# Moving two late x products and three y@w_ch products in a fused attention and spectral-mix kernel

## The chip, the cores and the metric

The kernel runs on one core of one Trainium2 chip. The time is the device time of one execution in microseconds (us). The profile's span is some 1.8 us shorter than the time of the same execution. All timed runs named here are of the same (fast) state, or single runs whose state isn't known; those are named.

The engines go by short names: PE multiplies matrices, DVE and ACT compute on and copy tiles (an *eviction* is a copy of a tile that PE wrote), POOL (GpSimd) issues the weight loads, SP the other DMAs. PE's granted clock is 1.00 or 0.50 in the records of these traces; 0.50 is called half clock. A load *lands* when its data are there.

## The reference, cut to what matters

```python
def reference(...):                      # q, k, v: (8, 8, 576, 64); w_r, w_i: (64, 512, 512); w_ch: (512, 512)
    x = attention(q, k, v, s)            # to (batch 8, sequence 576, 512)
    X = rfft(x, axis=1)[:, :64]          # 64 modes
    Y = X * (w_r + i w_i), mode by mode  # 64 products of (8, 512) by (512, 512), complex
    y = irfft(Y, n=576, axis=1)
    u = x + y
    return u + max(u @ w_ch, 0)
```

The product u @ w_ch is split: x @ w_ch and y @ w_ch. The second is cheap before the inverse transform, since Y has only 2 x 64 rows for each batch.

## The kernel before

The weights w_r and w_i (81.8 MB with q, k and v) are loaded on GpSimd's queue in 128 loads of 512 KB (as they land), and the last group of them is worked off in eight chunks of eight modes, four loads each. After each chunk its Y (`yb`, 128 rows: 16 of each of 8 batches) is transposed. Then there is a tail: for each pair of row tiles, the inverse transform of Y and of Y @ w_ch is added to x and to x @ w_ch. For that, both have to be laid out by batch in `yv`. That is done in two ways: by matmuls that pick one batch's columns out of the transposed Y (`gather`), or by a copy on SP (`spread`, 128 KB).

```python
    def spread(c, which, rows):
        nc.sync.dma_start(out=yv[16 * c : 16 * c + 16, :, which, :], in_=rows)
    # ... in modes(): for the last two chunks  spread(c, 0, yb)

    def y_times_wch(c, yt):
        # four matmuls 128x512 into v_ps, one DVE copy to v_sb
        spread(c, 1, vb)
        return vb

    def gather(c0, c1, turns, kinds):
        n = 2 * MC * (c1 - c0)               # 64 rows for four chunks, 32 for two
        ng = P // n                          # 2 or 4 batches share a PSUM tile
        for b0 in range(0, B, ng):
            for which in kinds:              # 1: @ w_ch, 0: as it is
                ps = auxpool.tile([P, DM], FP32, name="g_ps", tag="aux")      # two buffers
                # ... matmuls, ng column groups at once
                for g in range(ng):
                    # ... odd g on VectorE, even g on ScalarE, into yv
            if b0 // ng in turns:
                work()

    def work():                              # one late x product
        # transposes the next pair of x tiles; multiplies the pair before it by w_ch and keeps it

    TAKE = (3, 2, 2, 0, 1, 1)                # late products in chunks 0 to 5
    # ...
    for c in range(NCK - 2):                 # chunks 0 to 5
        yb = modes(NG - 1, c)
        for x in range(TAKE[c] - 1):
            work()
        # ...
        yt = y_transposed(yb, c)
        if TAKE[c]:
            work()
        if c >= NY:                          # chunks 4 and 5
            y_times_wch(c, yt)
            if c == NCK - 3:
                gather(NY, NCK - 2, (), (0,))
        elif c == NY - 1:                    # chunk 3
            gather(0, NY, (1, 3), (1, 0))
    # ... chunk 6: modes, transposes, vb6 = y_times_wch(6, yt)
    # ... chunk 7: modes, with the first pair's matmuls between its four loads
    # ... tail: 18 pairs; the third is the first to need all of yv
```

The softmax here doesn't subtract the row's maximum and nothing guards it: scores larger than these inputs give would overflow.

## Time and profile before

| | us |
|---|---|
| median of 3 runs | 456.54 (456.02 to 457.24) |
| span of the profiled execution | 453.8 |
| last weight load lands | 415.2 |
| chunk 7's last four mode products start | 415.30 |
| from there to the end | 38.5 |

The page names the engines' busy time, the chain that ended last, and the DMA queues. The prediction shows the lines on which its argument rests. Three lines of the page that it did not use are shown here, since they also belong here: the first, with the number of instructions, and two of the part on queues (packets, megabytes, share of the engines).

```profile
span 453.8 us, 10370 instructions
...
q8 instruction: 33, 0.54, 0.4%
q14 instruction: 14, 0.11, 0.1%
```

The program itself is read by DMA, in 33 packets of 16 KB on one queue and 14 of 8 KB on another. This is 0.5% of the engines' time and looks like nothing.

The next two lines are of the view of the tile `yv`, for the last copy of a v (chunk 7's): the issue (minimum, median and maximum in ns, then its time) and its time to landing.

```profile
L466 SPq DMA_DIRECT2D yv<-v_sb x1: 547/547/547, 418.7 to 418.7; - x1
...
DMA to landing us min/median/max: 2.9/2.9/2.9
```

### The profile page before, as it was taken

The page shows a single profiled execution, that of the slowest core. Times are in us where ns is not written, and L with a number is a line of the kernel's source. Part 1 is how long each engine was busy: PE and PEld are TensorE (multiplying, and loading weights), DVE is VectorE, ACT ScalarE, POOL GpSimd, SP SyncE. Part 2 cuts the span into 40 slices and gives each one's busy share as a digit, 9 for nine tenths or more (in the row PEclk, how much of TensorE's full clock was granted, in tenths as well). Part 3 has the DMA queues.
Part 4 walks back from the last instruction along what each step waited for, and adds up shares of the span by engine and source line. Part 5 has one row for each costly group of instructions (what it writes and reads, how often), then busy time and mean ns, then how long its engine had stood idle before and what let it go on. Part 6 is the DMA issues. An engine that isn't in the chain of part 4 may idle for free.

```text
span 453.8 us, 10370 instructions
## 1 busy us (share of the span) xinstructions
PE 340.4 (75%) x4233; PEld 218.6 (48%) x4265; DVE 241.0 (53%) x535; ACT 221.9 (49%) x390; POOL 183.0 (40%) x269
## 2 busy tenths in 40 slices
PE   1779887976563979836677857688889678879995
PEld 1456665654342656624445535456554335534332
DVE  7775665753242656723436434446655443562796
ACT  1585877464242656724435444455551323431774
POOL 6655554554344565434364444444433231200000
PEclk9996999998576889968878899889996986999999
DMA  9999999999999999999999999999999999995688
GB/s 176 200 203 203 202 201 204 202 204 204 205 204 202 201 203 202 205 205 204 202 196 203 204 204 203 204 203 202 206 207 208 207 206 206 207 214 109 232 298 317
DMA packets 108511, 93.75 MB, mean 207 GB/s; under 512 B 28384, under 2 KB 103648, under 8 KB 108464
## 3 DMA queue, kind: packets, MB, share of 16 engines
q0 software_dynamic: 98960, 81.81, 113.8%
q1 hardware_dynamic: 9504, 11.29, 7.8%
q8 instruction: 33, 0.54, 0.4%
q14 instruction: 14, 0.11, 0.1%
HBM read 164.56 MB, written 9.44 MB: 383 GB/s over the span
## 4 chain that ended last, share of the span: by engine, by line
DMA 51%; PE 31%; DVE 8%; issue 4%; POOL 2%; ACT 2%; SPq 0%; DVEq 0%; POOLq 0%; ACTq 0%
DMA w_sb<-in_moe_w_i_dram 21%; DMA q<-in_q_dram 15%; DMA w_sb<-in_moe_w_r_dram 11%; PE sc_ps L365 4%; PE av_ps L394 4%; PE z_ps L602 3%; PE yp L441 3%; PE sc_ps L359 3%; PE tr_ps L324 3%; DMA k<-in_k_dram 2%; PE z_ps L693 2%; PE g_ps L652 2%; PE ft_ps L418 2%; PE u_ps L712 2%; PE u_ps L693 1%
## 5 line engine op out<-in xcount | busy, mean ns | idle before, releaser
L373 ACT ACTIVATE p_sb<-sc_ps,cumt_sb 128x576 f16<-128x576 f32 (+1 forms) x256 | 141.7, 635 | 45.6 <-PE sc_ps L365 45.0
L217 POOL DMA_DIRECT2D w_sb<-in_moe_w_i_dram x60 | 45.1, 751 | 85.0 <-PE yp L441 37.6
L217 POOL DMA_DIRECT2D w_sb<-in_moe_w_r_dram x60 | 45.3, 757 | 63.5 <-DMA w_sb<-in_moe_w_r_dram 28.2
L217 POOL DMA_DIRECT2D v<-in_v_dram x72 | 50.8, 708 | 32.0 <-DMA w_sb<-in_moe_w_r_dram 7.4
L324 PE MATMUL tr_ps<-ident,q 64*64 64x64 bf16 x576 | 17.5, 210 | 54.3 <-DMA q<-in_q_dram 54.3
L359 PE MATMUL sc_ps<-negm,ident 128*128 128x256 bf16 x256 | 55.5, 303 | 0.2
L327 DVE COPY qtA<-tr_ps 64x576 bf16<-64x576 bf16 x32 | 23.8, 743 | 49.6 <-PE tr_ps L324 49.5
L441 PE MATMUL yp<-w_sb,xs 128*32 128x512 bf16 x480 | 36.5, 406 | 14.1 <-DMA w_sb<-in_moe_w_i_dram 11.1
L344 ACT ACTIVATE p<-sc_ps,cumt 128x64 f16<-128x64 f32 x32 | 10.0, 313 | 74.3 <-PE sc_ps L340 74.3
L394 PE MATMUL av_ps<-v,p_sb 128*128 128x65 f16 x1024 | 44.5, 198 | 0.0
L394 PEld LDWEIGHTS <-p_sb 128*128 128x128 f16 x1024 | 39.5, 100 | 4.9 <-issue 0.8
L327 DVE COPY ktA<-tr_ps 64x576 bf16<-64x576 bf16 x32 | 24.0, 749 | 33.6 <-PE tr_ps L324 33.6
L324 PEld LDWEIGHTS <-q 64*64 64x64 bf16 x576 | 13.7, 123 | 57.0 <-DMA q<-in_q_dram 56.3
L365 PE MATMUL sc_ps<-qtB,ktB 128*128 128x64 bf16 (+2 forms) x160 | 34.9, 324 | 3.5 <-issue 2.4
L365 PE MATMUL sc_ps<-qtA,ktA 65*128 65x512 bf16 (+2 forms) x192 | 36.5, 299 | 0.7 <-DMA qtA<-ncum_sb 0.7
L399 DVE TENSOR_REDUCE den<-av_ps 128x5 f32<-128x10 f32 x64 | 10.8, 169 | 49.1 <-PE av_ps L394 48.9
L441 PEld LDWEIGHTS <-xs 128*32 128x32 bf16 x512 | 22.6, 170 | 23.8 <-issue 19.8
L404 DVE TENSOR_TENSOR x_all<-av_ps,rcp 128x320 f16<-128x320 f32 x64 | 31.5, 491 | 2.2
L327 ACT COPY ktB<-tr_ps 64x576 bf16<-64x576 bf16 x32 | 20.3, 634 | 20.3 <-DVE ktA L327 19.4
L365 PEld LDWEIGHTS <-ktB 128*128 128x128 bf16 x192 | 22.4, 117 | 14.8 <-issue 6.3
L324 PE MATMUL tr_ps<-ident,k 64*64 64x64 bf16 x576 | 17.3, 209 | 15.3 <-DVE qtB L327 10.7
L602 PE MATMUL z_ps<-wch_sb,xs 128*128 128x512 f16 x96 | 26.1, 421 | 0.2 <-DVE xs L596 0.2
(117 smaller groups left out, 534.8 us busy)
## 6 DMA issues: line engine op xcount, KB each, us to landing
w_sb<-in_moe_w_r_dram POOLq DMA_DIRECT2D x60, 512.0 KB, 11.9
w_sb<-in_moe_w_i_dram POOLq DMA_DIRECT2D x60, 512.0 KB, 11.9
q<-in_q_dram POOLq DMA_DIRECT2D x32, 144.0 KB, 9.9
k<-in_k_dram POOLq DMA_DIRECT2D x32, 144.0 KB, 10.0
v<-in_v_dram POOLq DMA_DIRECT2D x72, 64.0 KB, 9.7
out_dram<-r_sb SPq DMA_DIRECT2D x16, 256.0 KB, 2.2
out_dram<-r_w SPq DMA_DIRECT2D x16, 256.0 KB, 2.6
x_all<-in_moe_w_i_dram POOLq DMA_DIRECT2D x3, 512.0 KB, 9.9
```

The costliest lines, as they stand in the source:

```text
L217: nc.gpsimd.dma_start(out=dst, in_=src)
L324: nc.tensor.transpose(ps[rows, r, :], src[rows, r, :], ident16[rows, rows])
L327: copy(out=dst[n % NQ][rows, :].rearrange("d (p r) -> d p r", r=R), in_=ps[rows].rearrange("d r p -> d p r"),)
L359: nc.tensor.matmul(ps[:, bass.ds(w * S, W)], ident16, negm[:, bass.ts(r, W)], start=True, stop=False, skip_group_check=True,)
L365: nc.tensor.matmul(ps[:, c0 : c0 + i1 - i0], keys[:, w, r, :], qt[:, i0:i1], start=False, stop=True, skip_group_check=True,)
L373: nc.scalar.activation(out=pt[:, poff[x] : poff[x] + S - w * W], in_=ps[:, w * S : (w + 1) * S - w * W], func=ACTF.Exp, bias=cumt_sb[:, x, ...
L394: nc.tensor.matmul(ps[:, I, r : r + NCH], lhsT, rhs, start=(i == 0), stop=(i == len(todo) - 1), skip_group_check=True,)
L399: nc.vector.tensor_reduce(out=den, in_=ps[:, :, 0 : VW : NCH], axis=mybir.AxisListType.X, op=ALU.add)
L404: nc.vector.tensor_tensor(out=x_all[:, g, b, :, D * h : D * h + D], in0=ps[:, :, 1 : NCH], in1=rcp.unsqueeze(2).to_broadcast([P, NT, D]), ...
L441: nc.tensor.matmul(ps[32 * cg : 32 * cg + 32, :], cols[:, c0 : c0 + 32, c * MC + 2 * cg + par], wt[(g, c, ri, par)][:, cg, :], start=(x == ...
L602: nc.tensor.matmul(z[:, x, :], xts[i][:, x, dt, :], wch_sb[:, dt, :], start=(dt == 0), stop=(last and dt == DT - 1), skip_group_check=True,)
L693: nc.tensor.matmul(dst[x][r, :], G_sb[rows, bass.ds(T * P, r.stop - r.start)], yv[rows, bb, which, :], start=start, stop=True, skip_group_ ...
```

## The change

It takes PE work off the stretch after the last chunks' loads, and copies off the stream of loads. (The change's title counts chunks from one; this text, like the code, from zero.) Two late x products move to chunks 0 and 1. The v of chunks 4 and 5 are gathered, like their y, in four column groups, with the rounds spread over the code. Chunk 6's v copy is issued behind chunk 7's y. In a gather, the last piece of a tile goes to DVE and all others to ACT.

```diff
@@ y_times_wch
-        spread(c, 1, vb)
         return vb
@@ gather(c0, c1, r, which): now one tile of one round
+        for g in range(ng):
+            dst, src = yv[rows, r * ng + g, which, :], ps[n * g : n * g + n, :]
+            if g == ng - 1:
+                nc.vector.tensor_copy(out=dst, in_=src)
+            else:
+                nc.scalar.copy(out=dst, in_=src)
@@
-    TAKE = (3, 2, 2, 0, 1, 1)
+    TAKE = (4, 3, 2, 0, 0, 1)
@@ for c in range(NCK - 2)
-        if c >= NY:
-            y_times_wch(c, yt)
-            if c == NCK - 3:
-                gather(NY, NCK - 2, (), (0,))
-        elif c == NY - 1:
-            gather(0, NY, (1, 3), (1, 0))
+        if c == NY - 1:
+            for r in range(4):
+                gather(0, NY, r, 1)
+                gather(0, NY, r, 0)
+                if r == 3:
+                    work()
+        elif c == NCK - 3:
+            gather(NY, NCK - 2, 0, 1)
+            gather(NY, NCK - 2, 0, 0)
     c = NCK - 2
     x_times_wch(0, False)
+    gather(NY, NCK - 2, 1, 1)
     yb6 = modes(NG - 1, c)
     x_transposed(1)
+    gather(NY, NCK - 2, 1, 0)
     # ...
     yb = modes(NG - 1, NCK - 1, {2: first_u, 3: first_z})
+    spread(NCK - 2, 1, vb6)
```

More of the change, by code (lines that the diff above doesn't have):

```diff
@@ L637, in y_times_wch, with gather @@
         nc.vector.tensor_copy(out=vb, in_=vp)
-        spread(c, 1, vb)
         return vb
-    def gather(c0, c1, turns, kinds):
+    def gather(c0, c1, r, which):
         n = 2 * MC * (c1 - c0)
@@ L645, in gather @@
         ng = P // n
-        for b0 in range(0, B, ng):
-            for which in kinds:
-                ps = auxpool.tile([P, DM], FP32, name="g_ps", tag="aux")
-                for dt in range(DT):
-                    for g in range(ng):
-                        op = yt_first[:, dt, : c1 - c0].rearrange("p c (x b) -> p (c x) b", b=B)
-                        nc.tensor.matmul(
-                            ps[n * g : n * g + n, :] if which else ps[n * g : n * g + n, bass.ts(dt, P)],
-                            op[:, :, b0 + g],
-                            wch_sb[:, dt, :] if which else ident16h,
-                            start=(dt == 0 or not which), stop=(dt == DT - 1 or not which),
-                            tile_position=(0, n * g), skip_group_check=True,
-                        )
-                for g in range(ng):
-                    dst, src = yv[rows, b0 + g, which, :], ps[n * g : n * g + n, :]
-                    if g % 2:
-                        nc.vector.tensor_copy(out=dst, in_=src)
-                    else:
-                        nc.scalar.copy(out=dst, in_=src)
-            if b0 // ng in turns:
-                work()
+        ps = auxpool.tile([P, DM], FP32, name="g_ps", tag="aux")
+        op = yt_first[:, :, : c1 - c0].rearrange("p d c (x b) -> p d (c x) b", b=B)
+        for dt in range(DT):
+            for g in range(ng):
+                nc.tensor.matmul(
+                    ps[n * g : n * g + n, :] if which else ps[n * g : n * g + n, bass.ts(dt, P)],
+                    op[:, dt, :, r * ng + g],
+                    wch_sb[:, dt, :] if which else ident16h,
+                    start=(dt == 0 or not which), stop=(dt == DT - 1 or not which),
+                    tile_position=(0, n * g), skip_group_check=True,
+                )
+        for g in range(ng):
+            dst, src = yv[rows, r * ng + g, which, :], ps[n * g : n * g + n, :]
[3 more added lines that the diff above has]
+                nc.scalar.copy(out=dst, in_=src)
     ahead = []
```

## The prediction

> **What bounds the kernel now.** I read the page's slices first, then the chain that ended last in order of time, then the issues of the weight loads with their time to landing, then the busy table in short windows.
>
> From the page, 40 slices of 11.3 us each:
>
> ```profile
> PE   1779887976563979836677857688889678879995
> PEclk9996999998576889968878899889996986999999
> GB/s 176 200 203 203 202 201 204 202 204 204 205 204 202 201 203 202 205 205 204 202 196 203 204 204 203 204 203 202 206 207 208 207 206 206 207 214 109 232 298 317
> ```
>
> The transfers run at a flat 200 to 208 GB/s for 36 slices while PE is never full. Only the last four slices (from 408 us) look different. So up to about 410 us the kernel is a stream of loads, then comes a tail without loads. The chain in order of time (start, length, what) gives another impression:
>
> ```profile
> 353.00 19.81 DMA w_sb<-in_moe_w_i_dram
> 372.80 0.04 issue
> 372.85 0.59 PE yp L441 x4
> ...
> 377.51 0.59 ACT yv L664
> 378.10 0.02 issue
> 378.12 0.70 DVE yv L662
> 378.83 0.04 issue
> 378.87 2.42 PE g_ps L652 x15
> ...
> 414.94 0.43 PE z_ps L702 x2
> 415.38 0.43 PE yp L441 x4
> ```
>
> After the load that landed at 372.8 the chain names no transfer any more: from there to the last chunk's last four matmuls (415.38) it is PE with ACT and DVE copies. Read alone, this says that all PE work after 372.8 us is on the path, and moving work ahead of it should pay in full. I do not believe that, because of the last loads. Issues on POOL, with start, length and idle time before:
>
> ```profile
> 391.58 0.74 POOL L217 DMA_DIRECT2D w_sb<-in_moe_w_i_dram  x1 [9.86 <-PE yp L441]
> 392.31 0.75 POOL L217 DMA_DIRECT2D w_sb<-in_moe_w_r_dram  x1
> 393.23 0.74 POOL L217 DMA_DIRECT2D w_sb<-in_moe_w_r_dram  x1 [0.17 <-PE yt_ps L625]
> 393.96 0.76 POOL L217 DMA_DIRECT2D w_sb<-in_moe_w_i_dram  x1
> 396.87 0.74 POOL L217 DMA_DIRECT2D w_sb<-in_moe_w_i_dram  x1 [2.15 <-PE yp L441]
> ```
>
> For the last one the tile view gives
>
> ```profile
> DMA to landing us min/median/max: 18.3/18.3/18.3
> ```
>
> so it lands at 396.87 + 18.3 = 415.17 us, and the first matmul that needs it starts at 415.30. Asked one by one, the last landings are 400.8 (issued 380.98 + 19.8), 404.3, 406.2, 409.3, 412.0 and 415.2. **Two paths meet at 415.2**: PE's own work, and the stream of loads. Taking work from PE alone gains almost nothing; the stream must shorten too.
>
> The POOL gap of 9.86 us looks alarming but starved nothing: four loads were still to land, and the windows table keeps its DMA share of 1.24 and 203 to 210 GB/s throughout the gap.
>
> **What the Trainium skill says.** "DMA: Bandwidth & Descriptors", section "Issuing engines are not separate DMA queues": transfers started from sync or gpsimd run on the same 16 DMA engines and interleave. So a copy of v into yv (128 KB, issued on SP) takes time from the weight stream. The trace agrees: undisturbed loads land 2.5 us apart (19.8 us latency, issues 2.53 us apart), but the last five took 415.2 - 400.8 = 14.4 us, not 5 x 2.53 = 12.65. In that time four such copies were in flight (issued 398.2, 402.6, 407.7, 411.9). That is 1.75 us for four, **0.44 us each**.
>
> "TensorE: Matmul & The Clock Gate", section "What's actually happening": PE runs at half clock after an idle activity window of about 3.4 us and at full clock after a busy one; the windows are free-running. The trace agrees. In windows of 1 us the granted clock is 0.50 from 342.3 to 349.1, 362.9 to 366.2 and 373.05 to 383.3; the edges all fit a period of 3.41 us. From 373 to 380 PE was some 59 and 71% busy (2.0 and 2.4 us of each window) and stayed slow; 379.9 to 383.3 was full (the late product at 381.3 filled it) and freed it.
>
> "PSUM — Partial Sum Buffer", section "PSUM bank collisions raise a hardware error": two engines must not touch the same bank and quadrant together; different quadrants may. The pieces of a gather are in different quadrants, but this kernel's DVE copies still follow the ACT ones (378.10, then 378.12), as the chain shows; I expect that order to stay.
>
> **The change part by part.** The instruction order before and after shows the same 247 GpSimd rows in the same order, so the loads themselves are unchanged; PE has 48 more (32 products and 32 weight loads added, 8 and 8 removed), SP two copies fewer.
>
> *Two late x products.* They go from the first gather (after r=1) and from chunk 4 to chunks 0 and 1. Each is 8 transposing matmuls (0.62 us) and 8 of 128x512 (1.73 us): 2.35 us at full clock. Before, PE sat idle around 359 to 363 and 371 to 373 us waiting for loads, so they fit there: chunk 1 ends at 357.9 + 4.7 = 362.6, and chunk 2's last load lands at 362.5. This may even spare the half clock at 362.9. Chunk 3 still ends with the load of 372.8. Off PE's path after 372.8: 4.7 us.
>
> *y@w_ch of chunks 4 and 5.* Removed: 2 x 4 matmuls (0.86 us each, 1.7 in all), two DVE copies of 0.69 and two SP copies. Added: two gathers of 16 matmuls of 128x32 weights, four column groups at once. The same form in the mode products costs 1.1 us for 16 (the timeline at 390.79: 1.12), so 2.2 us. Evictions: the gather of these chunks had two tiles with four pieces each, half on ACT and half on DVE; now it has four tiles, with three pieces of each on ACT and one on DVE: 3 x 0.58 + 0.70 = 2.4 us per tile, with two tiles in rotation. The four tiles cost about 9.7 us of copying between 398 and 409 us, mostly beside x products and waits. PE: +0.5 us. **Stream: two copies fewer.**
>
> *Chunk 6's v copy* (called chunk seven in the title, counting from one) now is issued behind y7's, after the last load. **One copy fewer ahead of the last landing.** Its consumer is the third pair's z at 421.99. The v7 copy, issued at 418.72, needs 2.9 us: 421.6. So there is only 0.35 us of slack, and an extra copy in flight could eat 0 to 0.3 us.
>
> *The stream's sum*: 3 x 0.44 = **1.3 us**. Last landing 415.2 - 1.3 = 413.9.
>
> *PE's sum*: 4.7 - 0.5 = 4.2 us less work, but not all is gained. With no product between its rounds the first gather waits for its copies. One round at full clock is 1.13 (PE) + 0.59 + 0.70 + 0.1 = 2.5 us; at half clock, as here from 373 us, about 3.4. Four rounds from 375.5: the last starts near 385.6 and its PE work ends at 388. In the windows 376.5 to 386.7 PE is then about 73% busy, as in the one that did not free the clock, so I expect half clock until about 390.1. Then the single product to 391.3, chunk 4 to 393.2, chunk 5 modes to 394.7 (before: 397.2), and carrying the rest on at full clock, with 2.4 us of eviction between gathers, PE is ready for the last four matmuls at about 413.5 (before: 415.3). So PE is ready about when the load lands, with little to spare.
>
> Sum: the end comes **1.3 us earlier, less 0.1** for the v copies: 456.54 - 1.2 = 455.3.
>
> **The rivals.**
>
> A: *PE is the bound, as the chain says.* Then 4.2 us less gives 452.3. For it: no transfer in the chain after 372.8. Against: the landing at 415.17 allows at most the shortening of the stream. I give it little.
>
> B: *A new PE delay.* The half clock holds longer (another 3.4 us window costs some 1.7 us), or ACT's twelve small evictions hold back the copy of chunk 6's transpose and so v6 and the first z. For it: my schedule has about 0.4 us of spare, and the windows' phase differs from run to run. It would make 455.5 to 457.5.
>
> C: *The copies were hidden.* The GB/s rose to 227 and 228 in the windows 402 to 404 and 406 to 408 us, so part of a copy is additional. Then the landing moves by only 0.5 us: 456.
>
> D: *Too much slack.* If PE idles over 2 us before the last load, the tail starts at half clock, +1.7 us. At 413.5 against 413.9 I don't expect it.
>
> **Range and chances.** The middle is 455.4, a little above the sum because B and C both push up. The copy's price alone (0.2 to 0.6 each) gives 454.7 to 456; B adds up to 2 us; the runs before spread by 1.2 us. Range 454.2 to 456.9. 2% is 9.1 us: faster would need more than all PE work moved, slower would need five extra half-clock windows.
>
> **What would show it.** Last weight landing at 413.5 to 414.3, and the last five landings 12.7 to 13.3 us apart in all. Chunk 4's mode products at 390 to 392 us with clock 0.5 up to about 390. PE waiting under 1 us for the last load, or the chain naming that load between 400 and 414. The stretch from the last mode matmul to the end unchanged at 38.0 us (415.81 to 453.8). The prediction is wrong if the last landing stays at 415 (C), if PE starts the last four over 0.5 us after their landing (B), or if the tail is longer than 38.4 us (the v copies).

## The result

The changed kernel took 457.26 us (median of 6 runs, 456.36 to 457.7), the kernel before 456.21 us on the same chip (6 runs, 455.56 to 457.24). The ratio is 1.0019, with a 95% interval of 1.0004 to 1.0035. A ratio is the mean time of one kernel's fast runs over that of the other's of the same rounds, so it is not quite the ratio of the medians. The change is within 2%, but it costs time, and the time lies above the range that was given.

The page after, its first line and three lines of its slices:

```profile
span 455.3 us, 10449 instructions
...
PE   1779997976553979836678788789888966889994
...
PEclk9995999997777799967769768799995995799999
...
GB/s 170 199 202 203 202 201 203 203 204 204 205 204 202 199 200 203 205 205 204 202 193 203 204 204 204 204 204 202 207 206 208 208 205 206 206 207 93 231 304 296
```

The page counts 79 instructions more; 32 of these are matmul records that are missing before (4233 matmuls against 4265 weight loads), and PE really has 48 more. The stream is as flat as before up to the 37th slice, in which it ends. The chain that ended last, in order of time:

```profile
386.63 2.42 PE g_ps L649 x14
389.06 0.97 PE xt_ps L592 x8
390.02 2.97 PE z_ps L602 x8
...
404.34 0.58 ACT yv L661
404.92 0.02 issue
404.94 0.71 DVE yv L659
405.65 0.04 issue
405.69 1.15 PE yp L441 x16
...
415.94 0.43 PE yp L441 x4
...
419.29 3.49 DMA yv<-v_sb
422.78 0.05 issue
422.83 0.60 PE z_ps L688 x2
```

Three things are new. The gather's last round starts at 386.6 and the product after it runs mostly at half clock (eight matmuls in 2.97 us; at full clock 1.73). Before chunk 6's mode products at 405.69 stand a row of ACT copies and a DVE copy, not a load. And after the last chunk the chain goes through the copy of v7, 3.49 us, where before it went through matmuls. The view of `yv` agrees; it gave 2.9 before:

```profile
DMA to landing us min/median/max: 3.5/3.5/3.5
```

The last load, from the issues on POOL and the view of its tile:

```profile
397.06 0.74 POOL L217 DMA_DIRECT2D w_sb<-in_moe_w_i_dram  x1 [0.22 <-issue]
...
DMA to landing us min/median/max: 18.0/18.0/18.0
```

It landed at 415.0 us, and the four matmuls that need it started at 415.87, where before the two were 0.1 us apart.

**Where the time went.** The landing records of the trace let the span be cut into five terms that don't depend on one another: until chunk 0's last load has landed (before any changed instruction), from there to the sixth landing from the end, the last five landings, the gap until the last four mode products start, and the rest.

| term, us | before | changed | difference |
|---|---|---|---|
| until chunk 0's last load | 342.16 | 343.30 | +1.14 |
| next 23 loads | 58.63 | 58.63 | 0.00 |
| last five loads | 14.42 | 13.08 | -1.34 |
| last landing to the last four products | 0.09 | 0.85 | +0.76 |
| tail, from these to the end | 38.50 | 39.43 | +0.93 |
| span | 453.8 | 455.3 | +1.5 |

Spans are rounded to 0.1 us, so the tails are good to 0.05.

The first term is before the change's first moved instruction. In the 14 profiles, all with the same loads up to there, it lies between 341.9 and 344.2 us. It is taken for scatter; whether any of it belongs to the change is open. (The profiled execution of the kernel before took 455.52 us, less than any of its six timed runs; that of the changed kernel took 457.06, near its median.) Without it the change cost 0.35 us here: it gained 1.34 us and lost 1.69.

### The profile page after: what moved, and what is told of

Read it like the earlier page. It is cut to its first block, busy times and chain, and to the rows that moved or that the text cites. A ratio compares the mean times of both kernels' runs of the same rounds, so it can differ in the third digit from the quotient of the medians.

```text
span 455.3 us, 10449 instructions
## 1 busy us (share of the span) xinstructions
PE 348.0 (76%) x4289; PEld 221.1 (49%) x4289; DVE 239.8 (53%) x533; ACT 227.0 (50%) x398; POOL 182.9 (40%) x269
## 4 chain that ended last, share of the span: by engine, by line
DMA 59%; PE 25%; DVE 6%; issue 5%; ACT 3%; POOL 2%; SPq 0%; DVEq 0%; POOLq 0%; ACTq 0%
DMA w_sb<-in_moe_w_i_dram 34%; DMA q<-in_q_dram 12%; DMA w_sb<-in_moe_w_r_dram 5%; DMA k<-in_k_dram 4%; PE sc_ps L365 3%; PE yp L441 3%; PE tr_ps L324 2%; PE av_ps L394 2%; PE sc_ps L359 2%; PE z_ps L688 2%; PE g_ps L649 2%; PE z_ps L602 1%; PE u_ps L707 1%; PE u_ps L688 1%; PE ft_ps L418 1%
## 5 line engine op out<-in xcount | busy, mean ns | idle before, releaser
L365 PE MATMUL sc_ps<-qtB,ktB 128*128 128x512 bf16 (+2 forms) x192 | 44.4, 348 | 0.0
```

Source lines behind the costliest of these rows:

```text
L365: nc.tensor.matmul(ps[:, c0 : c0 + i1 - i0], keys[:, w, r, :], qt[:, i0:i1], start=False, stop=True, skip_group_check=True,)
```

## The experiments

Twelve kernels ran. All gave the correct result. Since the first term scatters by over 2 us, the terms of the profile tell more than the times. The table has them, the sections after it what they mean. "Before" in the last columns is the kernel before in the same rounds; kernels without an interval had a single run.

| run | last five | gap | tail | median | before | ratio (95%) |
|---|---|---|---|---|---|---|
| kernel before | 14.42 | 0.09 | 38.50 | | | |
| changed | 13.08 | 0.85 | 39.43 | 457.26 | 456.21 | 1.0019 (1.0004 to 1.0035) |
| b1_take_only | 14.31 | 0.04 | 38.43 | 457.03 | 456.56 | 1.0017 (0.9999 to 1.0035) |
| a2_work_r1 | 13.09 | 0.23 | 39.84 | 457.23 | 456.56 | 1.0012 (0.9994 to 1.0030) |
| a1_v6_early | 13.48 | 0.04 | 39.41 | 456.91 | 456.56 | 1.0006 (0.9992 to 1.0021) |
| a3_no_gather45 | 14.29 | 0.38 | 38.44 | 456.22 | 456.56 | 0.9990 (0.9977 to 1.0003) |
| c4_split | 13.08 | 0.04 | 39.72 | 456.94 | 455.97 | |
| c1_fetch_both | 13.60 | 0.05 | 39.05 | 455.72 | 455.97 | 0.9992 (0.9973 to 1.0011) |
| c2_fetch_pe | 13.99 | 0.05 | 39.10 | 455.83 | 455.97 | |
| c3_fetch_sp | 13.34 | 0.20 | 39.44 | 456.55 | 455.97 | |
| e1_fetch_sp6 | 13.09 | 0.63 | 38.76 | 456.46 | 456.25 | |
| e4_before_pe | 14.35 | 0.04 | 38.84 | 456.19 | 456.25 | |
| e2_split_fetch | 13.09 | 0.04 | 39.10 | 455.83 | 456.25 | 0.9995 (0.9982 to 1.0007) |
| e3_all | 12.69 | 0.25 | 40.15 | 455.93 | 456.25 | 0.9991 (0.9978 to 1.0004) |

The theory at the start had three parts: the copies out of the stream gain 1.3 us; PE comes late, by the half clock and the evictions; and the late v6 copy beside it makes the v7 copy late. The rivals were that PE is the bound anyway, and that the clock alone, or the evictions alone, make PE late.

### The copies in the stream

Two runs put copies back.

a1_v6_early:

```diff
     vb6 = y_times_wch(c, yt)
+    spread(c, 1, vb6)
 ...
-    spread(NCK - 2, 1, vb6)
```

> The changed kernel with chunk 6's v copied right after its product again, ahead of the last load. Theory (PE is 0.8 us behind the stream, and the late copy makes the v7 copy land 0.6 us too late for the third pair): the 0.60 us wait for the v7 copy goes, the last landing moves by some 0.4 us without any effect, and the time falls by 0.3 to 0.6 us against 457.26. Rival (the stream sets the end): the time rises by about 0.4 us.

a3_no_gather45:

```diff
-        elif c == NCK - 3:
-            gather(NY, NCK - 2, 0, 1)
-            gather(NY, NCK - 2, 0, 0)
+        if c >= NY:
+            vb = y_times_wch(c, yt)
+            spread(c, 1, vb)
+            if c == NCK - 3:
+                for r in range(2):
+                    gather(NY, NCK - 2, r, 0)
 ...
-    gather(NY, NCK - 2, 1, 1)
-    gather(NY, NCK - 2, 1, 0)
```

> The changed kernel with the v products of chunks 4 and 5 as before the change (a product and an SP copy each). Theory (twelve ACT evictions in a row delay chunk 6's mode products from about 404.6 to 405.7 us): chunk 6's modes start when their last load lands, PE is ready for the last four about 1 us earlier, but the stream is 0.9 us longer for two copies, so the last four start at about the landing and the time is within 0.4 us of 457.26. Rival (the gather costs PE nothing): time 0.5 to 0.9 us above it, by the two copies in the stream.

Five loads without a copy should take 5 x 2.53 = 12.65 us. The runs give 12.69 with none (e3_all), 13.08 or 13.09 with one (the changed kernel, a2, c4, e1 and e2), 13.48 with two (a1), 14.29 with three (a3) and 14.31 to 14.42 with four. That is 0.4 to 0.5 us for a copy on average. Three runs with one copy don't fit: 13.34 (c3), 13.60 (c1) and 13.99 us (c2), for a cause that is left open. So the 1.3 us that the prediction gave this term is right in the profiled pair, while over all runs with one copy the gain against the kernel before lies between 0.43 and 1.34 us.

In a1 the gap went to 0.04 us, so it was PE that had been late. Its time, 456.91 us, lies in the range that was expected of it, but not for the reason given: what it was made for failed. The chain of a1 has the v7 copy as slow as before, with v6 out of its way:

```profile
419.69 3.52 DMA yv<-v_sb
423.21 0.05 issue
423.25 0.60 PE z_ps L688 x2
```

And a3, which has the late v6 copy, has no such wait, and a tail of 38.44 us. (Its time, 456.22 us, is 1.0 us below the changed kernel's, where at most 0.4 was expected.) **The theory of the two copies side by side fell.** What the long tails had in common was the gather of chunks 4 and 5, which has nothing to do with that copy, except that it makes the program longer on PE and shorter on SP.

### The half clock and the evictions

a2_work_r1 puts one of the moved products back into the first gather:

```diff
-    TAKE = (4, 3, 2, 0, 0, 1)
+    TAKE = (3, 3, 2, 0, 0, 1)
 ...
-                if r == 3:
+                if r in (1, 3):
```

> The changed kernel, but one of the two late x products goes back between the second and third round of the first gather (as before the change); the other stays moved. Theory (the gather without a product leaves PE at half clock): the clock is free again by about 385 us instead of 392.3, chunk 4's mode products start about 1 us earlier than the changed kernel's 392.9, the last four mode products start within 0.3 us of the last load's landing, and the time is 0.6 to 1.0 us below the changed kernel's 457.26 (so about that of the kernel before). Rival (the evictions by ACT at 401 to 407 us hold PE, whatever the clock): chunk 4 may come earlier, but the last four start as late after the landing as in the changed kernel (0.8 us), and the time stays within 0.3 us of 457.26.

In windows of 2 us (busy times and instructions of PE, its weight loads, DVE, ACT and POOL, then the granted clock, the DMA share and GB/s), first the changed kernel, then a2:

```profile
384.00:386.00 2.00, 1.69 (x14) 1.25 (x11) 0.11 (x1) 0.72 (x2) 0.00 (x0) 0.50 1.24 206
390.00:392.00 2.00, 2.00 (x7) 0.65 (x5) 1.85 (x3) 0.00 (x0) 0.00 (x0) 0.50 1.24 205
392.00:394.00 2.00, 2.00 (x20) 0.85 (x18) 0.00 (x0) 0.99 (x1) 0.31 (x1) 0.91 1.24 205
```

```profile
382.00:384.00 2.00, 2.00 (x12) 1.11 (x11) 1.97 (x4) 0.31 (x1) 0.00 (x0) 0.74 1.24 206
384.00:386.00 2.00, 2.00 (x19) 1.47 (x18) 0.48 (x1) 1.28 (x2) 0.00 (x0) 1.00 1.25 207
```

With the product between its rounds PE is full from 382 us and has its full clock at 383, as in the kernel before; without it, at 392.4. The product costs more PE work after the load of chunk 3, and yet the gap fell from 0.85 to 0.23 us. So a product that fills a gap came nearly free, and taking it away gained nothing. The time did not show it (457.23 us; 0.6 to 1.0 us less than 457.26 was expected): in the profile a tail of 39.84 us took back 0.4 of these 0.6 us, and the timed runs spread over 2.7 us.

c4_split leaves the clock alone and changes one line of the gather:

```diff
-            if g == ng - 1:
+            if not which:
                 nc.vector.tensor_copy(out=dst, in_=src)
```

> The changed kernel, but each gather's v tile is copied out by ACT alone and its y tile by DVE alone, so that the two run beside each other. Theory (PE is late for the last load because of evictions in series and the half clock): chunk 6's mode products start within 0.3 us of their last load instead of 1.2, and the last four start 0.0 to 0.3 us after the last landing instead of 0.85. Rival (only the half clock matters): still 0.6 us or more after it. Tail 39.4 us as in the changed kernel.

Now the v tile goes out by ACT alone and the y tile by DVE alone. The timeline of c4_split around the second gather:

```profile
400.37 2.34 ACT L661 CAST yv<-g_ps 32x512 f16<-32x512 f32 x4
400.60 2.79 DVE L659 CAST yv<-g_ps 32x512 f16<-32x512 f32 x4 [2.29 <-PE g_ps L649]
...
403.62 1.09 PE L441 MATMUL yp<-w_sb,xs 128*32 128x512 bf16 x16
```

The two tiles need 3 us side by side. In the changed kernel they and the next tile were one row of nine ACT copies, with DVE waiting behind:

```profile
401.39 5.41 ACT L661 CAST yv<-g_ps 32x512 f16<-32x512 f32 x9
...
405.69 1.13 PE L441 MATMUL yp<-w_sb,xs 128*32 128x512 bf16 x16 [0.68 <-DVE yv L659]
```

There chunk 6's mode products started at 405.69, 1.24 us after their last load had landed (404.45). Here they start at 403.62 and wait for no copy. The gap fell to 0.04 us, although the half clock lasted until 391.4. Both causes are real: the two delays are in one row. The split alone took away the whole gap, the earlier clock all but 0.2 us of it. The gap also moved by itself, with the very same PE code from the first gather on: 0.85 and 0.63 us where the clock came free at 392.4 and 392.2 (changed, e1), 0.20 where it came at 389.9 (c3; 0.26 us of that difference is its longer stream).

b1_take_only is the kernel before with the products alone moved:

```diff
-    TAKE = (3, 2, 2, 0, 1, 1)
+    TAKE = (4, 3, 2, 0, 0, 1)
 ...
-            gather(0, NY, (1, 3), (1, 0))
+            gather(0, NY, (3,), (1, 0))
```

> The kernel before with nothing but the two late x products moved to the first two chunks. Theory: half clock lasts till about 392 us as in the changed kernel, the landing stays at 71.2 to 72.3 us after the first y (as before), PE is a little earlier or as late, and the time is 0 to 0.5 us above the kernel before. Rival (PE is the bound, as its chain reads): 4.7 us less PE work, so 2 us or more below the kernel before.

It took 4.7 us of PE work from the chain and gained nothing: 1.0017, last five 14.31 us, gap 0.04, tail 38.43. So the rival that takes the chain at its word is out. The clock came free at 391.8 us here.

### The tail: the program's own instructions

The trace's records of single DMA packets show what the page only counts. The 16 KB packets on queue 8 started, counted from the start of the last four mode products, at +8.3 us before and at +4.6 us after the change. The v7 copy runs from +3.4 to +6.9. Before, all 16 engines finished that copy within 0.3 us; after, 15 of them within 0.2 us and the last one 0.7 us later. The 8 KB packets on queue 14 show the same for the last output stores:

```text
                     16 KB (queue 8)    8 KB (queue 14)   last engine late by, us
                     after last four    after last four   v7 copy    last 5 stores
kernel before             +8.3              +31.6          none       none
changed                   +4.6              +34.0          0.7        0.5
a1_v6_early               +4.4              +34.0          0.7        0.5
a2_work_r1                +4.5              +34.4          1.0        0.6
c4_split                  +4.4              +34.3          1.0        0.6
a3_no_gather45            +9.5              +31.7          none       none
b1_take_only              +8.2              +31.7          none       none
c1_fetch_both             +9.4              +33.1          none       0.5
c2_fetch_pe               +9.4              +33.7          none       0.5
c3_fetch_sp               +4.4              +33.5          0.8        0.4
e1_fetch_sp6              +4.5              +29.6          0.7        0.3 or less
e4_before_pe              +4.4              +32.1          0.8        none
```

("Late" is how long after the other 15 the last of the 16 engines reported, by the semaphore updates that each landing leaves.) The new theory: these are fetches of instructions, queue 8 for PE, the last block on queue 14 for SP. (An 8 KB packet some 22 us after the last four stays there in all runs, whatever SP's instructions; it may be another engine's.) The change gives PE 48 instructions more, so its next block is due earlier; it gives SP two copies fewer, so its next block is due later. Each fetch holds up one of the 16 engines (the records don't say which engine took a packet; this is argued from the one in 16 that is late), and a copy is there only when its last engine is. The Trainium skill has the mechanism in "Runtime: NRT & Kernel Launch", section "Instruction fetch mechanics": an engine's instructions are refilled in blocks of 16 KiB (256 instructions) by a DMA queue of its own, and the cost of crossing a block is one tail-bump, "mostly hidden". The counts agree: 4265 weight loads on the page before, with a matmul each, are 8530 instructions; over 256 that is 33.3 blocks, and the page has 33 packets. The 8 KB blocks of queue 14 aren't in that section.

Five runs test it. c1_fetch_both, c2_fetch_pe and c3_fetch_sp add instructions that change no result, far ahead in the attention phase:

```diff
@@ c1 and c2: in fft(n), 104 times in all
+        for _ in range(4 if n < 8 else 3):
+            nc.tensor.matmul(ps, x_all[:, g, b, 0, :], Ff_sb[:, 0, :], start=True, stop=True)
@@ c1 and c3: in the attention loop
             cum_rows(n + 1)
+            if n == 8:
+                cum_rows(n + 1)
```

> The changed kernel with 104 redundant matmuls (208 PE instructions with their weight loads) spread over the attention phase and two tiny copies on SP issued twice; the output is the same. Theory (two instruction fetches of the program itself fall on the v7 copy and on the last output stores, because the change made PE 48 instructions longer and SP two copies shorter): the 16 KB fetch moves from 4.6 us after the last four mode products to about 8.2 us, as before the change, and the later 8 KB fetch from 34.0 to 31.6; the 0.6 us wait for the v7 copy and the late last stores go, so the tail (from the start of the last four mode products to the end) is 38.5 us, not 39.4, and the time falls by 0.9 us. Rival (the v7 copy is slow because v6 is in flight beside it): the tail stays at 39.4 us.

> Only the 104 redundant matmuls. Theory: the 16 KB fetch moves to about 8.2 us after the last four, the wait for v7 goes, the last stores stay late: tail about 39.1 us. Rival (the fetch has nothing to do with the wait): tail 39.4 with the wait of 0.6 us.

> Only the two repeated SP copies. Theory: the 8 KB fetch moves from 34.0 to 31.6 us after the last four, no engine is late on the last five output stores, the v7 wait stays: tail about 38.8 us. Rival: tail 39.4.

The PE half holds in both runs: the fetch moved to +9.4 us, the wait for v7 went, and the tail was 39.05 and 39.10 us, as was expected of c2. But it did not come free: it is in these two runs that the last five loads took 13.60 and 13.99 us. The fetch now started 6 to 7 us after the sixth landing from the end, beside chunk 6's y copy; in the other runs with one copy in the stream it came at 0.4 to 2.5 us there. Whether that is the cause wasn't tested. Here is c2's v7 copy:

```profile
DMA to landing us min/median/max: 2.9/2.9/2.9
```

The SP half was no test: two repeated tiny copies moved the 8 KB fetch by 0.5 us only, and it still met the last stores. So c1 and c3 missed what was expected of the tail. e1_fetch_sp6 repeats them six times:

```diff
             cum_rows(n + 1)
+            for _ in range(6 if n == 8 else 0):
+                cum_rows(n + 1)
```

> The changed kernel with six repeats (twelve tiny copies) on SP; the repeat of two copies moved the 8 KB fetch by only 0.5 us, too little to test. Theory (that fetch falls on the last output stores): it moves by about 3 us, from 34.0 to 31 us after the last four mode products, the engine that is 0.5 us late on the last stores is gone, and the tail is 38.8 us instead of 39.4, with the wait for v7 still there. Rival (the late stores have another cause): tail 39.4.

Its tail is 38.76 us (38.8 expected), with the v7 wait still in it. e4_before_pe goes the other way: the kernel before, with 48 PE instructions more and nothing else.

```diff
@@ in fft(n), 24 times in all
+        for _ in range(1 if n < 24 else 0):
+            nc.tensor.matmul(ps, x_all[:, g, b, 0, :], Ff_sb[:, 0, :], start=True, stop=True)
```

> The kernel before with nothing but 24 redundant matmuls (48 PE instructions, as many as the change adds). Theory (the 16 KB fetch of PE's instructions): the fetch moves from 8.3 to about 4.6 us after the last four mode products, the copy of v7 takes 3.5 us instead of 2.9, the chain names a wait for it, and the tail is 38.8 us instead of 38.5. Rival (the wait comes from v6 beside it): tail 38.5, no wait.

The chain of e4_before_pe:

```profile
418.95 3.63 DMA yv<-v_sb
422.58 0.05 issue
422.63 0.60 PE z_ps L695 x2
```

The kernel before now has the wait of the changed one, and a tail of 38.84 us (38.8 expected). Of the 0.93 us that the tail grew, PE's fetch makes some 0.3 us (39.43 against 39.10 in c2; 38.84 against 38.50 in e4) and SP's some 0.65 us (39.43 against 38.76 in e1). These are single profiles; with the fetches in the same places the tail was 39.41 to 39.44 us in the changed kernel, a1 and c3, but 39.84 in a2 and 39.72 in c4, where the late engine of v7 was 1.0 us late.

### All cures together

e2_split_fetch is the changed kernel with c4's split, 20 redundant matmuls and e1's copies. e3_all has also a2's product back in the gather and issues chunk 6's y copy behind the last load.

```diff
@@ e3, on top of e2
-            if c >= NCK - 2:
+            if c == NCK - 1:
                 spread(c, 0, yb)
 ...
+    spread(NCK - 2, 0, yb6)
     spread(NCK - 2, 1, vb6)
```

> The changed kernel with the gathers' evictions split by tile between ACT and DVE, 20 redundant matmuls (40 PE instructions) and twelve tiny SP copies. Theory: last five loads 13.1 us, last four at most 0.2 us after the landing, no v7 wait (the 16 KB fetch falls near 2 us after the last four, before v7 is issued), tail 38.5 us: from chunk 0's last landing to the end 110.2 us against 111.6 in the kernel before, so some 1.4 us (0.3%) faster than it. Rival (something else still holds it): no more than 0.5 us faster.

> As e2_split_fetch, with one late product back in the first gather and chunk 6's y copy issued behind the last load too. Theory: last five loads 12.65 us, PE still in time because the clock is free 8 us earlier, tail 38.5: 109.8 us from chunk 0's last landing, 1.8 us (0.4%) faster than the kernel before. Rival (four copies in flight together delay the third pair, or PE cannot keep up): the 0.4 us come back as a wait for a yv copy or as a gap after the last landing.

Both missed. In e2 the stream, the gap and the v7 copy are as expected, but the 40 PE instructions brought one more 16 KB fetch into the tail (at +27.4 us), and from about 3 us after it one engine was 0.6 us or more late on every store to the end: tail 39.10 us instead of 38.5. In e3 the stream is at its 12.69 us, and the rest comes back in the tail. With three copies between the last load and v7, and a fetch at +2.3 us, v7 took

```profile
417.94 4.00 DMA yv<-v_sb
```

and the tail 40.15 us. Here it was not one engine: 15 of the 16 were there 1.1 us later than in the kernel before, with v7 issued 0.3 us later, and the last one another 0.3 us after them. So three copies ahead of v7 do delay it, where one more (the changed kernel against a1) did not. The times are 0.9995 and 0.9991 of the kernel before, with intervals that hold 1: no version was shown to beat the kernel before. The 14.42 - 12.69 = 1.7 us (an estimate from the terms) that all gains without a fetch in the wrong place would save were not reached.

## Why the prediction was wrong

By its own steps:

- *Two paths meet at 415.2, and the stream must shorten too*: right. b1 takes the work off PE alone and gains nothing.
- *The stream's sum, 3 x 0.44 = 1.3 us*: right, 1.34 us in the profiled pair (three other runs with one copy gained less). The landing came at 415.02; less the shift of the first term, 1.14 us, that is 413.9, as predicted.
- *POOL's gap starves nothing*: right. The gap is 10.83 us after the change, and the 23 loads took 58.63 us in both.
- *PE's sum, "PE is ready for the last four matmuls at about 413.5"*: wrong by size. It allowed for the half clock until 390.1 us and for the evictions, but put the first landing term aside; with that added (1.14 us) it says 414.6, and PE was ready at 415.87. Of its pieces the clock (free at 392.4, so 391.2 less the shift) was missed by 1.1 us, and the row of ACT copies, which it called "mostly beside x products and waits", kept chunk 6's mode products waiting for 1.24 us (rival B had named the copy of chunk 6's transpose instead). This is rival B, against which it had 0.4 us of spare; it cost 0.76 us, and the gap of 0.85 us is over the 0.5 that the prediction named as the sign of B.
- ***"Sum: the end comes 1.3 us earlier, less 0.1 for the v copies"*: this is the step that failed.** The tail was not 0.1 us longer but 0.93. The prediction counted the 48 PE instructions more and the two SP copies fewer, and gave them no cost beyond their own time. Their cost was that they moved two instruction fetches of the program onto the v7 copy and onto the last stores. It did see that v7 had only 0.35 us of slack, and that a tail over 38.4 us would be a sign (its tail starts at the end of the last mode product, and went from 38.0 to 38.9 us); the reason that it gave (v6 in flight beside v7) is refuted by a1 and a3.
- *Rival C (the copies were hidden) and D (a cold tail)*: neither. The clock was 1.00 from 392.4 to 453.8 us.
- One sum is off, and nothing rests on it: five half-clock windows at 1.7 us each are 8.5 us, not the 9.1 us and more that "slower" would need.

That the time lies in rival B's range (455.5 to 457.5) is partly luck: B explains 0.76 us of it, and the tail, which no rival had for its true reason, 0.93.

In the profiled pair, -1.34 + 0.76 + 0.93 = +0.35 us. The timed ratio of 1.0019 is +0.9 us with an interval of 0.2 to 1.6, which holds 0.35. The rest may be the scatter of the first term, or be due to the change; this is left open. So is what makes that scatter. In four of the runs (c1, c4, e1, e2) the 23 loads took 0.4 to 1.1 us longer, each time by one step between 347 and 364 us. Each step came 2 to 3 us after a 16 KB packet on queue 8, but other runs have such packets there without a step.

## What to carry to other kernels

When a chain of waits names only compute after some point, look up when the last load lands before counting compute as gain: here both ended within 0.1 us, and only the shorter stream could pay. A gap that one engine fills for free (a product while PE waits for evictions) can be worth more there than elsewhere, since it also brings back the full clock (383 against 392.4 us here). And a tail with little slack should be checked for the program's own fetches: 48 PE instructions more in the attention phase moved a fetch onto a copy that the tail waits for (e4), so a change of 1 us can be covered by where a block boundary happens to fall.

## What the Trainium skill lacked or had wrong

- "Runtime: NRT & Kernel Launch", section "Instruction fetch mechanics": it calls the cost of crossing a 16 KiB block "mostly hidden". The fetch also takes one of the 16 DMA engines from the kernel's own transfers: the v7 copy took 3.5 us instead of 2.9, and 48 redundant PE instructions alone made the tail 38.84 us instead of 38.50 (e4). The section says nothing of this, nor of the 8 KB blocks seen on queue 14.
- "DMA: Bandwidth & Descriptors", section "Issuing engines are not separate DMA queues": it says that transfers interleave but gives no price. Here a copy of 128 KB within the stream cost it 0.4 to 0.5 us on average (12.69 us for five loads with none, 13.08 or 13.09 with one in five runs, 13.48 with two, 14.29 with three), with three runs above that (13.34 to 13.99 with one).
- "TensorE: Matmul & The Clock Gate", section "What's actually happening": it doesn't say how busy a window has to be to count as busy. Here windows of 3.41 us in which PE was about 72% busy by the profile did not free the clock (376.5 to 379.9 before the change), and a full one did (379.9 to 383.3).
